# Sparse attention and two feed-forward layers on one core: tying every instruction to its place in the recorded plan

## Chip, cores and metric

The kernel runs on one core of a Trainium2 chip. The metric is the device time of one execution in microseconds (us). The engines are called as the profile calls them: PE (TensorE), ACT (ScalarE), DVE (VectorE), POOL (GpSimd) and SP (SyncE, which here only issues DMA).

## What is computed

The reference takes q, k, v of shape 4 x 8 x 576 x 64 (batches, heads, positions, width) and four weight matrices. Cut to what matters:

```python
scores = np.matmul(q, k.transpose(0, 1, 3, 2)) / np.sqrt(D)
kth = np.partition(scores, -32, axis=-1)[..., -32:-31]       # 32nd largest of each row
scores = np.where(scores >= kth, scores, -1e9)
attn = softmax(scores)
x = (attn @ v), heads side by side                           # 2304 x 512
h = x @ moe_w_in;   x = np.maximum(0.01 * h, h) @ moe_w_out  # 512 -> 2048 -> 512
h = x @ moe2_w_in;  out = (h * sigmoid(h)) @ moe2_w_out
```

## The kernel before

The 2304 tokens are cut into 18 blocks of 128 rows (two of them join the 64 last rows of two batches). In each block the eight heads are done as four pairs, so there are 72 pairs.

One pair goes through all engines in turn. PE multiplies q and k (`S`, line 727); ACT copies the scores out of PSUM (`s_copy`, tile `sb`, line 739); DVE finds the 32nd largest value of each row by seven steps for each of two heads (`chain`, lines 753 to 757: maximum of eight, replace them, and again); ACT masks (`cut`, 779), takes the exponential (`exp`, 788) and writes an fp16 copy (`p_hi`, tile `ph`, 803); POOL writes the rest that fp16 lost (`p_lo`, 811); SP issues a transposing DMA (`ptr`, tile `pT`, 820); PE multiplies with v (`pv`, 841). There are two `sb` buffers, one `ph`, one `pT` and one PSUM tile `S`, so a step waits for a step of an earlier pair that still holds its buffer.

After two pairs ACT and DVE combine the halves of `pv` (`comb_a`, 875, and `comb_b`, 880), and POOL scales them (`comb_c`, 887). After four pairs the block is a row of x, is split into fp16 high and low parts and transposed (`xhi`, `xlo`, `xtr`). Each of the two layers then makes four quanta `h` for a block, of 12 matmuls each (963). A quantum of layer 0 is read by ACT (`g0`, 974); one of layer 1 by ACT (`g1`, a tanh, 976) and then by DVE (`g2`, 981). There are two PSUM tiles `h`, so PE's next quantum waits until one was read. `ghi` (ACT, 990), `glo` (POOL, 997) and `gtr` (SP, 1002) make the transposed input of four quanta `o` (1016), which add up in PSUM tile `acc` (two of them). Layer 0's `acc` becomes y (`ysq`, `yhi`, `ylo`, `ytr`); layer 1's is scaled by ACT (`of`, 1029) and stored. The q and k, v tiles of later pairs are loaded and split on the way (`qsq`, `qsc`, `qhi`, `qtr` and others). In the first 250 us the four weight matrices are also turned from fp64 into two fp16 parts, on DVE, ACT and POOL (`wz`, `wsign`, `wmid`, `wjoin`, `whi`, `wlo`).

What sets the order: each step is an `Op` with its engine and an estimated duration, recorded by `Plan.add`. `Plan.run` (below) schedules all of them by a list scheduler with its own clocks and yields `order`. Its last two lines call every step's function in that order, which traces the instructions:

```python
        for o in order:
            o.fn()
```

That is not yet the order on the engines. When the `TileContext` is closed, the framework's own scheduler goes over the traced instructions. [...]

Of the kernel before, what the change touches and what calls it, by code (L numbers as in the profile page):

```python
# [64 lines left out]
STATS = {}  # L65


class Op:
    __slots__ = ("n", "eng", "dur", "lat", "dma", "fn", "new", "use", "pred", "succ", "bl", "left", "ready", "t0", "t1", "name", "soft", "stage", "slot")


class Plan:
# [5 lines left out]

    def __init__(self):
        self.ops = []
        self.writer = {}
        self.readers = defaultdict(list)
        self.tag = {}
        self.users = defaultdict(list)
        self.last = {}
        self.named = {}

    def add(self, eng, dur, fn, r=(), w=(), new=(), lat=0.0, dma=0.0, seq=None, name="", after=(), mark=None, soft=None, stage=None):  # L90
        o = Op()
        o.n, o.eng, o.dur, o.lat, o.dma, o.fn, o.name = len(self.ops), eng, dur, lat, dma, fn, name
        o.pred, o.succ, o.new, o.use = {}, [], list(new), set()
        for tag, key in new:
            self.tag[key] = tag
        for x in r:
            if x in self.writer:
                o.pred[self.writer[x]] = True
            self.readers[x].append(o)
        for x in w:  # L100
            if x in self.writer:
                o.pred[self.writer[x]] = True
            for y in self.readers[x]:
                if y is not o:
                    o.pred[y] = True
            self.readers[x] = []
            self.writer[x] = o
        for x in list(r) + list(w):
            key = x[0] if isinstance(x[0], tuple) else x
            if key in self.tag and o not in self.users[key]:  # L110
                self.users[key].append(o)
                o.use.add(key)
        for p in after:
            if p in self.named:
                o.pred.setdefault(self.named[p], False)
        if mark is not None:
            self.named[mark] = o
        if seq is not None:
            if seq in self.last:
                o.pred.setdefault(self.last[seq], False)  # L120
            self.last[seq] = o
        o.soft, o.stage, o.slot = None, stage, ()
        if soft is not None:
            if soft in self.last:
                self.last[soft].soft = o
            self.last[soft] = o
        self.ops.append(o)
        return o

    def run(self):  # L130
# [20 lines left out]
        order = []  # L151
# [5 lines left out]
        while len(order) < total:  # L157
            best = None
            for e in engines:
# [25 lines left out]
                x = min((x for x in lst if x[0] <= t0 + SLACK[e]), key=lambda x: (-x[1].bl - BOOST.get(x[1].name, 0), x[1].n))  # L185
# [4 lines left out]
            _, o, t = best  # L190
# [43 lines left out]
                    cand[s.eng].append(s)  # L234
            order.append(o)
        STATS.update(order=order, busy=busy, span=max(o.t1 for o in order))
        for o in order:
            o.fn()


def stages(nb):

    out = []
    for b in range(nb + LEAD):
        if b < nb:
            out.append((0, b))
        if b >= LEAD:
            out.append((1, b - LEAD))
    return out
# [3 lines left out]
def topk_attention_moe_moe2_kernel(  # L253
# [52 lines left out]
    for s in range(NS):  # L306
        blk, p = divmod(s, NP)
        for _, _, b, _ in blocks[blk]:
            first_use.setdefault((b, p), s)

    plan = Plan()
    add = plan.add
    T = {}

# [58 lines left out]
    def w_ops(i):  # L373
# [3 lines left out]
        for c in range(NWP):  # L377
# [3 lines left out]
            for o, n in units:  # L381
# [12 lines left out]
                def load(o=o, n=n, c=c, small=small, rk=rk, raw=raw):  # L394
# [4 lines left out]
                    nc.sync.dma_start(out=dst, in_=w_rows(i, c, o, n))  # L399

                add("SP", 0.55, load, w=rnames, new=rnew, lat=1.8, dma=3.0 * n / WP, name=f"wload{i}", seq="wload",
                    after=W_AFTER if i == 0 and c == 0 else ())

# [3 lines left out]

                zn = [yslot, (yslot, o)] if small else [yslot]
                add("ACT", act_t(n, 1), z, r=rnames, w=zn, name=f"wz{i}")
                m = n if i < 3 else min(n, 512)  # L410
                for o2 in range(0, n, m):
# [12 lines left out]
                    def sign(o2=o2, m=m, tk=tk, t_of=t_of, raw=raw):  # L424
# [8 lines left out]
                        else:  # L433
                            nc.vector.tensor_scalar(u[:, :, 1], s16[:, o2:o2 + m], 32768, None, op0=ALU.bitwise_and)

                    add(W_SIGN[i], {"DVE": 0.08 + 0.65 * m / WP, "POOL": POOL_TS * m / WP}[W_SIGN[i]], sign, r=rnames, w=tn, new=tnew, name=f"wsign{i}")

                    def mid(o2=o2, m=m, t_of=t_of, raw=raw):
# [604 lines left out]
    order = stages(NB)  # L1043
# [62 lines left out]
```

## Time and profile before

| | |
|---|---|
| median of three runs | 1258.48 us (1257.63 to 1261.75) |
| the profiled execution, its own time | 1260.39 us |
| its span, first to last instruction | 1258.6 us |
| busy, share of the span: PE, DVE, ACT, POOL | 81%, 74%, 66%, 49% |
| mean granted TensorE clock | 0.906 |

The span is 1.8 us under the execution's own time. A busy share is an average over stages: the last 150 us are PE alone, the first 250 us are mostly DVE and ACT. An engine runs its instructions in the order in which they stand, so a wait of one instruction is a wait of all behind it; what matters is what stands there.

### The profile page before, as it was taken

How to read it: one execution, taken by the hardware profiler on the slowest of the kernel's cores; microseconds unless marked ns; L12 is line 12 of the kernel's file. 1: busy time of each engine (PE TensorE's matmuls, PEld its weight loads, DVE VectorE, ACT ScalarE, POOL GpSimd, SP SyncE). 2: the span in 40 equal slices, each digit the busy share in tenths (PEclk: the TensorE clock that was granted, in tenths of full speed). 3: DMA queues.
4: the chain of work that ended last, by engine and by line, in shares of the span. 5: the costliest groups of instructions: out<-in, count | busy, mean ns of one | idle time of the engine just before them, and what ended most of it. 6: DMA issues, size and time to landing. Idle time of an engine off the chain costs nothing.

```text
span 1258.6 us, 18096 instructions
## 1 busy us (share of the span) xinstructions
PE 1020.8 (81%) x6024; PEld 503.6 (40%) x6024; DVE 935.6 (74%) x1906; ACT 836.5 (66%) x1408; POOL 616.3 (49%) x864
## 2 busy tenths in 40 slices
PE   3324275798898998897988988989997998999988
PEld 1223133343444443343444433445443443444433
DVE  6989999998749899788788877873988787920000
ACT  6898998887658775676777666665767655642222
POOL 2333455775636554555554645555555544542221
PEclk9555578798999999899989988999999999999989
DMA  8988855456756656467665637565566555553232
GB/s 226 280 247 279 242 135 110 92 97 134 123 117 124 121 117 99 87 123 141 132 111 109 123 73 131 106 132 120 91 118 115 86 100 100 108 114 67 51 74 52
DMA packets 458110, 157.44 MB, mean 125 GB/s; under 512 B 440864, under 2 KB 449056, under 8 KB 455968
## 3 DMA queue, kind: packets, MB, share of 16 engines
q1 hardware_dynamic: 458016, 156.29, 59.7%
q8 instruction: 47, 0.77, 0.3%
q14 instruction: 47, 0.39, 0.1%
HBM read 47.71 MB, written 4.72 MB: 42 GB/s over the span
## 4 chain that ended last, share of the span: by engine, by line
PE 30%; DVE 12%; POOL 10%; DMA 10%; ACT 9%; issue 8%; SPq 1%; POOLq 0%; ACTq 0%; DVEq 0%
PE acc L1016 13%; PE h L963 13%; DMA pT<-ph 5%; DVE w L755 5%; POOL ph L811 5%; DVE m L757 3%; DMA gT<-hl 3%; PE pv L841 2%; ACT sb L739 2%; POOL hl L997 2%; PE S L727 2%; DVE m L753 2%; ACT sb L788 2%; ACT sb L779 1%; ACT ph L803 1%
## 5 line engine op out<-in xcount | busy, mean ns | idle before, releaser
L1016 PE MATMUL acc<-w_all,gT 128*128 128x512 f16 x1728 | 410.7, 390 | 34.0 <-ACT of L1029 19.7
L757 DVE MAX8 m<-w 128x8 f32<-128x576 f32 x432 | 309.6, 749 | 0.1
L997 POOL TENSOR_TENSOR hl<-g,hl 128x512 f16<-128x512 f32 x144 | 168.8, 1173 | 230.5 <-ACT hl L990 208.6
L1016 PEld LDWEIGHTS <-gT 128*128 128x128 f16 x1728 | 168.9, 100 | 239.1 <-issue 52.9
L811 POOL TENSOR_TENSOR ph<-sb,ph 128x1152 f16<-128x1152 f32 x72 | 171.5, 2382 | 129.2 <-ACT ph L803 115.9
L963 PE MATMUL h<-w_all,xT 128*128 128x512 f16 x864 | 207.9, 394 | 21.2 <-ACT g L974 16.7
L963 PE MATMUL h<-w_all,yT 128*128 128x512 f16 x864 | 203.6, 388 | 17.3 <-DVE g L981 15.9
L755 DVE MATCH_REPLACE8 w<-m,w 128x576 f32<-128x576 f32 x288 | 212.4, 743 | 0.0
L753 DVE MAX8 m<-sb 128x8 f32<-128x576 f32 x144 | 103.3, 750 | 76.1 <-ACT sb L739 76.0
L981 DVE SCALAR_TENSOR_TENSOR g<-g,h 128x512 f32<-128x512 f32 x72 | 49.1, 682 | 139.8 <-ACT g L976 139.8
L990 ACT ACTIVATE hl<-g 128x512 f16<-128x512 f32 x144 | 89.7, 624 | 75.4 <-DMA gT<-hl 65.2
L963 PEld LDWEIGHTS <-xT 128*128 128x128 f16 x864 | 86.5, 101 | 128.3 <-issue 34.3
L963 PEld LDWEIGHTS <-yT 128*128 128x128 f16 x864 | 85.7, 100 | 121.3 <-issue 26.7
L739 ACT ACTIVATE sb<-S 128x1152 f32<-128x1152 f32 x72 | 81.2, 1127 | 78.8 <-POOL ph L811 75.8
L727 PE MATMUL S<-k,qT 128*128 128x64 f16 (+3 forms) x640 | 95.8, 309 | 44.2 <-ACT sb L739 37.1
L779 ACT ACTIVATE sb<-sb,m 128x576 f32<-128x576 f32 x144 | 106.1, 766 | 33.2 <-DVE m L757 33.1
L788 ACT ACTIVATE sb<-sb,nb,u 128x576 f32<-128x576 f32 x144 | 123.3, 858 | 5.0 <-POOL nb L767 4.6
L841 PE MATMUL pv<-v,pT 128*128 128x128 f16 (+3 forms) x1600 | 111.7, 213 | 13.8 <-DMA pT<-ph 13.8
L803 ACT ACTIVATE ph<-sb 128x1152 f16<-128x1152 f32 x72 | 83.2, 1156 | 50.5 <-DMA pT<-ph 50.5
L841 PEld LDWEIGHTS <-pT 128*128 128x128 f16 (+3 forms) x1600 | 86.1, 102 | 52.9 <-DMA pT<-ph 18.9
L755 DVE MATCH_REPLACE8 w<-m,sb 128x576 f32<-128x576 f32 x144 | 106.0, 743 | 0.0
L472 PE MATMUL acc<-w_all 128*128 128x128 bf16 x256 | 31.7, 295 | 73.8 <-DVE w_all L455 69.5
(94 smaller groups left out, 1088.4 us busy)
## 6 DMA issues: line engine op xcount, KB each, us to landing
w_all<-in_moe_w_in_dram SPq DMA_DIRECT2D x16, 1024.0 KB, 6.5
w_all<-in_moe_w_out_dram SPq DMA_DIRECT2D x14, 1024.0 KB, 5.1
raw<-in_k_dram SPq DMA_DIRECT2D x16, 256.0 KB, 3.1
rawq<-in_q_dram SPq DMA_DIRECT2D x32, 128.0 KB, 2.8
raw<-in_v_dram SPq DMA_DIRECT2D x16, 256.0 KB, 3.0
out_dram<-of SPq DMA_DIRECT2D x16, 256.0 KB, 2.3
gT<-hl SPq DMA_TRANSPOSE x144, 3.2
of<-in_moe_w_out_dram SPq DMA_DIRECT2D x8, 256.0 KB, 2.8
```

The source lines that it names most:

```text
L727: nc.tensor.matmul(out=t[p0:p1, o:o + k1 - k0], lhsT=lhs, rhs=kt[:, k0:k1], start=(x == 0), stop=(x == 1),)
L739: nc.scalar.activation(out=T[sbk], in_=src, func=AF.Copy)
L753: nc.vector.max(m[:, 0], T[sbk][:, h])
L755: nc.vector.match_replace(w, m[:, step // 2], T[sbk][:, h] if step == 1 else w, NEG)
L757: nc.vector.max(m[:, step // 2], w)
L779: nc.scalar.activation(out=x, in_=x, func=AF.Prelu, scale=-1.0, bias=T["m", s][:, h, 3, 7:8], alpha=2.0**-CUT)
L788: nc.scalar.activation(out=x, in_=x, func=AF.Exp, scale=T["u", blk, hf][:, 1, p % 2:p % 2 + 1], bias=T["nb", s][:, h:h + 1], accum_out=T[" ...
L811: nc.gpsimd.tensor_tensor(out=T[phk][:, 1, x0 * S:x1 * S], in0=T[sbk][:, x0:x1].rearrange("p h k -> p (h k)"), in1=T[phk][:, 0, x0 * S:x1 ...
L841: nc.tensor.matmul(out=o[p0:p1, h, p % 2, 0:n], lhsT=l, rhs=r, start=(i == 0), stop=(i == len(mm) - 1))
L963: nc.tensor.matmul(out=t, lhsT=a[:, ai], rhs=w_rhs(layer, wi, kk, i), start=(n == 0), stop=(n == 3 * KDM - 1))
L997: nc.gpsimd.tensor_tensor(out=n[:, 1], in0=T[gk], in1=n[:, 0], op=ALU.subtract)
L1016: nc.tensor.matmul(out=t, lhsT=g[:, ai], rhs=w_rhs2(layer, wi, 4 * i + j), start=(i == 0 and j == 0 and n == 0), stop=(i == NCH - 1 and j ...
```

## The change

Each traced instruction gets a manual dependency on the instruction that was traced before it on the same engine (`add_manual_dep`, class `NoSync`). Both are on one engine, which keeps their order anyway, so the dependency needs no semaphore: it only binds the framework's scheduler. `use` of an `Op` becomes a list in place of a set. The whole diff:

```diff
--- before.py
+++ after.py
@@ -65,6 +65,9 @@
 STATS = {}
 
 
+ORDER = mybir.DependencyInfo(mybir.DependencyClass.NoSync, mybir.DependencyReason.DATA)
+
+
 class Op:
     __slots__ = ("n", "eng", "dur", "lat", "dma", "fn", "new", "use", "pred", "succ", "bl", "left", "ready", "t0", "t1", "name", "soft", "stage", "slot")
 
@@ -78,7 +81,8 @@
 
 
 
-    def __init__(self):
+    def __init__(self, tc):
+        self.tc = tc
         self.ops = []
         self.writer = {}
         self.readers = defaultdict(list)
@@ -90,7 +94,7 @@
     def add(self, eng, dur, fn, r=(), w=(), new=(), lat=0.0, dma=0.0, seq=None, name="", after=(), mark=None, soft=None, stage=None):
         o = Op()
         o.n, o.eng, o.dur, o.lat, o.dma, o.fn, o.name = len(self.ops), eng, dur, lat, dma, fn, name
-        o.pred, o.succ, o.new, o.use = {}, [], list(new), set()
+        o.pred, o.succ, o.new, o.use = {}, [], list(new), []
         for tag, key in new:
             self.tag[key] = tag
         for x in r:
@@ -109,7 +113,7 @@
             key = x[0] if isinstance(x[0], tuple) else x
             if key in self.tag and o not in self.users[key]:
                 self.users[key].append(o)
-                o.use.add(key)
+                o.use.append(key)
         for p in after:
             if p in self.named:
                 o.pred.setdefault(self.named[p], False)
@@ -234,8 +238,16 @@
                     cand[s.eng].append(s)
             order.append(o)
         STATS.update(order=order, busy=busy, span=max(o.t1 for o in order))
+        behind = {}
         for o in order:
+            traced = self.tc.nc.cur_bb.bb.instructions
+            n = len(traced)
             o.fn()
+            for x in self.tc.nc.cur_bb.bb.instructions[n:]:
+                p = behind.get(x.engine)
+                if p is not None:
+                    self.tc.add_manual_dep(x, p, ORDER, reason="order of issue")
+                behind[x.engine] = x.name
 
 
 def stages(nb):
@@ -308,7 +320,7 @@
         for _, _, b, _ in blocks[blk]:
             first_use.setdefault((b, p), s)
 
-    plan = Plan()
+    plan = Plan(tc)
     add = plan.add
     T = {}
```

No instruction is added or taken away. Names of buffers carry the numbers that tracing gave them; they are the same in both programs, so the plan is the same. In the program of before the engines' order differs from the plan; in the changed one it is the plan. PE's order is nearly the same in both from the end of the weight work on: of its 11942 rows 11003 stand at the same place. On ACT, DVE, POOL and SP most places differ. Lines of the changed kernel are 12 higher in this part (739 becomes 751).

**First place, ACT and DVE in block 13 of layer 1.** ACT before; `g_10495` is `g1` of the layer's first quantum of that block, read from PSUM tile `h_10427`, and `xf_10509` is `comb_a`:

```order
L739 ACTIVATE sb_10471<-S_10385 128x1152
L779 ACTIVATE sb_10362<-sb_10362,m8_10402 128x576 x2
L788 ACTIVATE sb_10362,rs_10002<-sb_10362,nb_10512,u_9631 128x576 x2
L990 ACTIVATE hl_10556<-g_10383 128x512
L990 ACTIVATE hl_10614<-g_10424 128x512
L976 ACTIVATE g_10495<-h_10427,u2_10274 128x512
L976 ACTIVATE g_10568<-h_10451,u2_10274 128x512
L875 ACTIVATE xf_10509<-pv_10310 128x256
```

And now:

```order
L751 ACTIVATE sb_10471<-S_10385 128x1152
L988 ACTIVATE g_10495<-h_10427,u2_10274 128x512
L887 ACTIVATE xf_10509<-pv_10310 128x256
L791 ACTIVATE sb_10362<-sb_10362,m8_10402 128x576 x2
L800 ACTIVATE sb_10362,rs_10002<-sb_10362,nb_10512,u_9631 128x576 x2
L1002 ACTIVATE hl_10556<-g_10383 128x512
L1041 ACTIVATE of_10560<-acc_10341,u2_9597 128x512
```

`g1` and `comb_a` stood behind two `cut`, two `exp` and two `ghi`, and now stand right behind `s_copy` (`sb_10471`). DVE there, before (`g_10495` is `g2`, `xf_10509` is `comb_b`, the rows on `m8_10534` are the chain of the next pair):

```order
L753 MAX m8_10534<-sb_10471 128x8 x2
L755 MATCH_REPLACE w_10535<-m8_10534,sb_10471 128x576 x2
L757 MAX m8_10534<-w_10535 128x8
L856 SCALAR_TENSOR_TENSOR den_10563<-rs_10002,sv3_78 128x4
L757 MAX m8_10534<-w_10535 128x8
L862 RECIPROCAL rec_10565<-den_10563 128x4
L755 MATCH_REPLACE w_10535<-m8_10534,w_10535 128x576 x2
L981 SCALAR_TENSOR_TENSOR g_10495<-g_10495,h_10427 128x512
L757 MAX m8_10534<-w_10535 128x8 x2
L755 MATCH_REPLACE w_10535<-m8_10534,w_10535 128x576
L981 SCALAR_TENSOR_TENSOR g_10568<-g_10568,h_10451 128x512
L880 TENSOR_TENSOR xf_10509<-pv_10310,xf_10509 128x256
```

And now:

```order
L993 SCALAR_TENSOR_TENSOR g_10495<-g_10495,h_10427 128x512
L892 TENSOR_TENSOR xf_10509<-pv_10310,xf_10509 128x256
L765 MAX m8_10534<-sb_10471 128x8 x2
L767 MATCH_REPLACE w_10535<-m8_10534,sb_10471 128x576 x2
L868 SCALAR_TENSOR_TENSOR den_10563<-rs_10002,sv3_78 128x4
L874 RECIPROCAL rec_10565<-den_10563 128x4
L769 MAX m8_10534<-w_10535 128x8 x2
L767 MATCH_REPLACE w_10535<-m8_10534,w_10535 128x576
L993 SCALAR_TENSOR_TENSOR g_10568<-g_10568,h_10451 128x512
L767 MATCH_REPLACE w_10535<-m8_10534,w_10535 128x576
L769 MAX m8_10534<-w_10535 128x8 x2
```

Both `g2` and `comb_b` stood inside the chain, and now stand ahead of its first row.

**Second place, ACT in block 9 of layer 0.** `g_7092` is the `g0` for which a quantum of `h` waits. Before (`xss_7035`, `hlx_7102` are `ysq`, `yhi`; `qss_7147` is `qsq`):

```order
L990 ACTIVATE hl_7196<-g_6909 128x512
L974 ACTIVATE g_6993<-h_6941 128x512
L901 ACTIVATE junk_69,xss_7035<-acc_6775 128x512
L650 ACTIVATE junk_69,qss_7147<-rawq_7067 128x256
L922 ACTIVATE hlx_7102<-acc_6775,ys_7054 128x512
L803 ACTIVATE ph_7128<-sb_6870 128x1152
L779 ACTIVATE sb_7014<-sb_7014,m8_7063 128x576 x2
L974 ACTIVATE g_7092<-h_7041 128x512
L739 ACTIVATE sb_7168<-S_7026 128x1152
```

And now:

```order
L751 ACTIVATE sb_7014<-S_6900 128x1152
L913 ACTIVATE junk_69,xss_7035<-acc_6775 128x512
L1002 ACTIVATE hl_7038<-g_6845 128x512
L791 ACTIVATE sb_6870<-sb_6870,m8_6931 128x576
L677 ACTIVATE rawq_6935<-rawq_6935,qs_7020 128x256
L791 ACTIVATE sb_6870<-sb_6870,m8_6931 128x576
L986 ACTIVATE g_7092<-h_7041 128x512
L800 ACTIVATE sb_6870,rs_6933<-sb_6870,nb_7090,u_6067 128x576
L934 ACTIVATE hlx_7102<-acc_6775,ys_7054 128x512
L800 ACTIVATE sb_6870,rs_6933<-sb_6870,nb_7090,u_6067 128x576
L815 ACTIVATE ph_7128<-sb_6870 128x1152
```

`g0` stood behind `ysq`, `qsq`, `yhi`, `p_hi` and the two `cut` of `sb_7014`. Of these only `ysq` is still ahead of it. It now stands right behind the `cut` of the pair before (`sb_6870`), and that pair's two `exp`, which ran long before it, stand behind it.

**Third place, SP in block 5.** `pT_4669` is the transpose `ptr` for which a `pv` waits. Before:

```order
L939 DMA_TRANSPOSE yT_4589<-hlx_4588 128x8x128
L1002 DMA_TRANSPOSE gT_4616<-hl_4615 128x8x128
L692 DMA_TRANSPOSE qT_4679<-hlx_4678 128x8x128
L820 DMA_TRANSPOSE pT_4669<-ph_4592 128x18x128
L1002 DMA_TRANSPOSE gT_4649<-hl_4648 128x8x128
L641 DMA rawq_4746<-in_q_dram 128x4x64
```

And now:

```order
L951 DMA_TRANSPOSE yT_4589<-hlx_4588 128x8x128
L832 DMA_TRANSPOSE pT_4669<-ph_4592 128x18x128
L1014 DMA_TRANSPOSE gT_4616<-hl_4615 128x8x128
L1014 DMA_TRANSPOSE gT_4649<-hl_4648 128x8x128
L704 DMA_TRANSPOSE qT_4679<-hlx_4678 128x8x128
L653 DMA rawq_4746<-in_q_dram 128x4x64
```

`ptr` stood behind a `gtr` (`gT_4616`) and a `qtr`; now it is ahead of both.

## Rows read from the trace of the kernel before

**Rows 1.** Busy time on the page: us (share of the span) xinstructions.

```profile
PE 1020.8 (81%) x6024; PEld 503.6 (40%) x6024; DVE 935.6 (74%) x1906; ACT 836.5 (66%) x1408; POOL 616.3 (49%) x864
```

**Rows 2.** Three stretches: length, busy us (instructions) by engine, granted clock, DMA share, GB/s.

```profile
0.00:250.00 250.00, 116.19 (x751) 69.29 (x752) 227.62 (x425) 214.88 (x311) 114.66 (x144) 0.69 0.73 202
250.00:1105.00 855.00, 760.84 (x4580) 368.87 (x4579) 692.03 (x1458) 576.82 (x1021) 462.83 (x671) 0.96 0.61 113
1105.00:1259.00 154.00, 143.81 (x697) 65.40 (x695) 15.92 (x26) 44.82 (x77) 38.77 (x49) 0.98 0.36 70
```

**Rows 3.** Waits of PE, 250 to 1105 us: us in total, times, longest us.

```profile
PE acc L1016 <- ACT of L1029: 19.7, 9, 5.7
PE h L963 <- ACT g L974: 16.7, 6, 5.8
PE h L963 <- DVE g L981: 15.9, 6, 5.8
PE S L727 <- ACT sb L739: 11.4, 11, 2.6
PE pv L841 <- DMA pT<-ph: 11.2, 7, 3.5
PE h L530 <- DVE g L981: 5.0, 1, 5.0
```

**Rows 4.** Timeline of ACT near 1053 us: start, us, instruction, [idle before <-releaser].

```profile
1052.41 1.13 ACT L739 ACTIVATE sb<-S 128x1152 f32<-128x1152 f32 x1 [1.66 <-POOL ph L811]
1053.44 1.43 ACT L779 ACTIVATE sb<-sb,m 128x576 f32<-128x576 f32 x2
1054.77 0.86 ACT L788 ACTIVATE sb<-sb,nb,u 128x576 f32<-128x576 f32 x1
...
1055.62 0.86 ACT L788 ACTIVATE sb<-sb,nb,u 128x576 f32<-128x576 f32 x1
...
1056.47 1.14 ACT L990 ACTIVATE hl<-g 128x512 f16<-128x512 f32 x2
1057.52 0.67 ACT L976 ACTIVATE g<-h,u 128x512 f32<-128x512 f32 x1
```

**Rows 5.** Timeline of PE in the same stretch.

```profile
1045.74 5.34 PE L963 MATMUL h<-w_all,yT 128*128 128x512 f16 x24
...
1060.00 1.33 PE L963 MATMUL h<-w_all,yT 128*128 128x512 f16 x4 [2.67 <-DVE g L981]
```

**Rows 6.** Timeline of ACT and PE near 730 us.

```profile
724.04 0.86 ACT L788 ACTIVATE sb<-sb,nb,u 128x576 f32<-128x576 f32 x1
...
724.50 5.34 PE L963 MATMUL h<-w_all,xT 128*128 128x512 f16 x24
...
733.26 0.69 ACT L922 ACTIVATE hlx<-acc,ys 128x512 f16<-128x512 f32 x1 [5.30 <-POOL ys L330]
...
734.90 1.43 ACT L779 ACTIVATE sb<-sb,m 128x576 f32<-128x576 f32 x2
...
736.23 0.58 ACT L974 ACTIVATE g<-h 128x512 f32<-128x512 f32 x1
...
736.86 4.15 PE L963 MATMUL h<-w_all,xT 128*128 128x512 f16 x12 [5.85 <-ACT g L974]
```

**Rows 7.** Timeline of the SP queue near 495 us.

```profile
494.58 1.23 SPq L1002 DMA_TRANSPOSE gT<-hl  x1
495.92 2.01 SPq L692 DMA_TRANSPOSE qT<-hlx  x1
498.03 3.19 SPq L820 DMA_TRANSPOSE pT<-ph  x1
```

**Rows 8.** Timeline of PE near 500 us.

```profile
502.72 1.33 PE L841 MATMUL pv<-v,pT 128*128 128x128 f16 x20 [3.55 <-DMA pT<-ph]
```

**Rows 9.** Waits of DVE, 250 to 1105 us.

```profile
DVE g L981 <- ACT g L976: 42.8, 18, 13.8
```

**Rows 10.** Waits of ACT, 250 to 1105 us.

```profile
ACT g L974 <- PE h L963: 10.0, 6, 4.2
```

## The prediction

> **What bounds the kernel now.** I read first the page's busy time, then the same by stage, then what PE waits for, then the order at the worst waits. On the page [rows 1] PE is busy for 1020.8 us of 1258.6, DVE for 935.6: no engine is full, so the shares alone do not tell the bound. The three stretches do [rows 2]. In the first 250 us DVE is busy for 227.6 and ACT for 214.9: the weights are made, and PE has little to do at a granted clock of 0.69. In the last 154 us PE is busy for 143.8 and DVE for 15.9: the attention is done, and PE works off what is left. Between them, 855 us, PE is busy for 760.8 and DVE for 692.0. What PE does not do in the middle it must do in the end, so PE's idle time of the middle, 855 - 760.8 = 94.2 us, is what a better order can win, as long as the chain on DVE keeps up; DVE has 855 - 692.0 = 163 us of slack there.
>
> The list of PE's waits in the middle [rows 3] says what the 94 us are. Most are not for data but for a place to write: PE waits for ACT to empty `acc` (`of`, 19.7 us in 9 waits), for ACT or DVE to empty an `h` tile (16.7 in 6, 15.9 in 6, and 5.0 once in front of a small matmul that takes an `h` tile too). That is 57.3 us in 22 waits. 11.2 us are waits for the transposed probabilities, 11.4 for `s_copy`.
>
> **What the order does there.** First place: PE ends two quanta of `h` at 1045.74 + 5.34 = 1051.1, so the first at about 1048.4, and stands still for 2.67 us until 1060.00, when `g2` has freed that tile [rows 5]. ACT could have run `g1` from 1048.4 on, but `s_copy`, two `cut`, two `exp` and two `ghi` stood ahead, and it ran at 1057.52 [rows 4]. Now it stands right behind `s_copy`, which ends at 1052.41 + 1.13 = 1053.5: four us earlier, more than the 2.67 that PE lost. On DVE `g2` now comes ahead of the next pair's chain, which starts later by about the two steps that moved.
>
> Second place: `g0` ran at 736.23 and PE waited 5.85 us for it [rows 6]. Its `h` was ready by 724.50 + 5.34 / 2 = 727.2; ACT then stood 5.30 us in front of `yhi`. Now `g0` is ahead of `yhi`, and the wait is gone. But its new place is ahead of an `exp` that ran at 724.04. At the times of this trace ACT would stand there for 727.2 - 724.04 = 3.2 us, with the pair's exponentials behind it. This is the price of the change, and it shows the risk.
>
> Third place: `ptr` was issued at 498.03, behind a `gtr` and a `qtr` of 1.23 and 2.01 us [rows 7], and PE waited 3.55 us for its landing [rows 8]. Now it goes ahead of both: 3.2 us earlier.
>
> **The change part by part.**
> - *Waits for a free PSUM tile*, 57.3 us [rows 3]. At two of two places read, the awaited step passes more work than PE lost. Yet these are the worst places of the old order, and a new one has worst places of its own. Bounds: 0 and -57.3. I take half: -28.7.
> - *Waits for `pT`*, 11.2 us [rows 3], by the third place: bounds 0 and -11.2, I take half: -5.6.
> - *The clock after a wait.* [...] Bounds: 0, and -34 us, the 0.04 that the middle's granted clock of 0.96 lacks [rows 2], times 855.
> - *New waits at the head of ACT and DVE.* They show already: DVE stood 42.8 us for `g1` [rows 9], ACT 10.0 us for `h` [rows 10], 52.8 together. PE-fed steps now stand earlier, so I let these waits double. What stands behind is the chain and its `cut` and `exp`; these reach PE as waits for `pT` and `s_copy`, 11.2 + 11.4 = 22.6 of PE's 94 us, a quarter. 52.8 / 4 = +13.2. Bounds: 0 and +52.8, all of it passed on.
> - *The first 250 us.* Weight steps on DVE move ahead of steps of the first chains. The same work runs on an engine busy for 227.6 of 250 us, so one gains what the other loses: 0, with DVE's idle 22 us [rows 2] as bound on either side.
> - *The last 154 us.* PE's order is unchanged and PE is busy for 143.8 [rows 2]: 0, at best -10.
> [...]
>
> Sum: -28.7 - 5.6 - 7.5 + 13.2 = -28.6 us. Against the profiled execution's own 1260.4 us this is 1231.8; that execution lies 1.9 us above the median of the runs, 1258.5, so I forecast **1230 us**.
>
> [...]
>
> **The rivals.**
> - *Slower: the heads block.* ACT and DVE start nothing ahead of the instruction at their head. In the middle some 15 blocks pass with eight `g`, two `comb_a` and one `of` each, 165 PE-fed steps on ACT, all with the pair's `cut` and `exp` behind them. If PE comes no earlier than in this trace, they wait as in the second place, there for 3.2 us. With 0.8 us on average ACT stands 132 us longer, of its idle 855 - 576.8 = 278 [rows 2]; half of it reaching the pair's loop is +66, less the 41.8 us won above: +24, **1283 us**. It decides from 0.5 us on average (165 x 0.5 / 2 = 41). For it: the 3.2 us, and 42.8 us that DVE stood in the same way [rows 9]. Against it: 10.0 us in 6 waits is all that ACT stood for layer 0's `h` [rows 10], and PE itself comes earlier when its tiles come free. [...]
> - *No change.* PE's order is nearly the same, and PE soon comes to the next `S` or `pv`, which hang on the chain. Then a wait for a free tile becomes a wait for `s_copy` or `pT`, and the time stays: **1258 us**. To the same comes the case that the change does not act: the framework's order might differ only where nobody waits. The three places speak against that.
> [...]
>
> **How the numbers follow.** Forecast (1205 to 1254): 0.53. Much faster: 0.11. No change: 0.11. Slower: 0.25. A measurement of this kernel tells about 0.3%, 3.8 us, from no change; the chances are faster 0.64, same 0.11, slower 0.25. The range leaves out half of the much faster case and about a half of the slower one, whose price grows with each tenth of a us of mean wait: 1193 to 1284 us.
>
> **What would show it.** Right: in the middle stretch PE's waits for `of`, `g0` and `g2` fall from 57 to about 30 us, its granted clock rises above 0.96, and the last chain ends before 1105 us. The new price: ACT's waits for `h` and DVE's for `g1` grow from 52.8 towards 100. Wrong: PE's idle time in the middle stays at 94 us and only changes its name to `s_copy` and `pT`, or ACT stands for `h` for well over 100 us and the chain ends after 1105.

## The result and the profile after

The changed kernel takes **1146.95 us** (median of four runs, 1143.96 to 1147.79) against 1258.18 us before (1257.63 to 1261.75): the ratio is 0.911, 95% interval 0.908 to 0.913. That is 111 us less, where the prediction had 28.6, and 46 us below its range. The sign was right, the size was not. The profiled execution took 1143.96 us with a span of 1142.2, 116.4 us under the span of before.

One thing stated ahead has to be put right: there is one PSUM tile `acc`, not two. So a wait for `of` is a wait for the only tile there is. Lines of the changed kernel are 12 higher: 963 is 975, 974 is 986, 976 is 988, 739 is 751.

The page's busy line after, to hold against [rows 1]:

```profile
PE 986.2 (86%) x6024; PEld 497.1 (44%) x6024; DVE 931.5 (82%) x1906; ACT 839.9 (74%) x1408; POOL 622.6 (55%) x864
```

The instructions are the same in number, and in both traces they run in the order of the built programs: all 1159 ACTIVATE rows of ACT and all 498 DMA issues of SP stand at their place. DVE, ACT and POOL need the same time for them within about 1%, PE 34.6 us less (1020.8 - 986.2). Now the three stretches after, cut where the last chain ends on DVE (before: 1105 us; now 997):

```profile
0.00:250.00 250.00, 112.24 (x735) 68.03 (x736) 225.72 (x421) 214.16 (x305) 119.53 (x142) 0.83 0.71 201
250.00:997.00 747.00, 736.87 (x4630) 366.54 (x4629) 691.02 (x1463) 583.74 (x1032) 465.80 (x677) 1.00 0.71 129
997.00:1143.00 146.00, 137.13 (x663) 62.49 (x660) 14.77 (x23) 42.01 (x73) 37.30 (x47) 1.00 0.37 72
```

Against [rows 2]: the first 250 us are as they were but for PE's granted clock there (0.69 before, 0.83 now), the last stretch is 8 us shorter, and the middle is 108 us shorter with the same work on DVE (692.0 and 691.0 us). In it PE is busy for 736.87 of 747 us, 98.6%, at a granted clock of 1.00, where it was 0.96 before. The 116.4 us of span can be written as PE's busy time plus its idle time by stretch (the end up to the last instruction):

| PE | before | after | difference |
|---|---|---|---|
| busy, all | 1020.8 | 986.2 | -34.6 |
| idle, first 250 us | 133.8 | 137.8 | +4.0 |
| idle, middle | 94.2 | 10.1 | -84.1 |
| idle, end | 9.8 | 8.1 | -1.7 |

What PE waits for in the middle, 250 to 997 us, to hold against [rows 3] (us in total, times, longest):

```profile
PE h L542 <- ACT junk L598: 3.2, 2, 2.8
PE acc L1028 <- ACT of L1041: 3.1, 2, 2.4
PE pv L853 <- DMA pT<-ph: 1.5, 2, 0.9
PE S L739 <- ACT sb L751: 1.3, 2, 1.1
```

The waits for `g0` and `g2` are gone from the list; 3.1 us for `of`, 1.5 for `pT` and 1.3 for `s_copy` are left. The price that the prediction looked for stands in the lists of DVE and ACT of the same stretch. DVE and ACT after:

```profile
DVE g L993 <- ACT g L988: 8.9, 13, 3.8
...
DVE m L765 <- ACT sb L751: 3.6, 5, 2.1
...
ACT sb L751 <- POOL ph L823: 38.8, 42, 2.0
ACT g L986 <- PE h L975: 25.0, 22, 3.9
ACT g L988 <- PE h L975: 22.0, 24, 3.5
...
ACT xf L887 <- PE pv L853: 11.3, 9, 2.2
```

ACT now stands for `h` 47.0 us (25.0 for `g0`, 22.0 for `g1`). Before it was 11.5: the 10.0 of [rows 10] are `g0` alone, and `g1` adds 1.5 (last line below). DVE stands for `g1` 8.9 us, not 42.8 [rows 9]. Some rows of before that the prediction did not read belong beside them (DVE and ACT, 250 to 1105 us):

```profile
DVE m L753 <- ACT sb L739: 73.9, 38, 5.8
...
ACT sb L739 <- POOL ph L811: 67.2, 45, 3.3
ACT ph L803 <- DMA pT<-ph: 50.0, 26, 4.8
...
ACT g L976 <- PE h L963: 1.5, 4, 0.7
```

DVE's wait for the scores at the head of the chain was the largest wait of DVE before, and fell from 73.9 to 3.6 us. The whole loop of a pair (`s_copy`, chain, `p_hi`, `p_lo`, `ptr`) became quicker, with every step as long as it was. That this one wait falls is no gain in itself, as the kernel with only DVE tied shows below.

The second place of the prediction shows how a new wait costs nothing. ACT and PE after, with the same `g0` (start, us, instruction, idle before it):

```profile
662.50 5.34 PE L975 MATMUL h<-w_all,xT 128*128 128x512 f16 x24
...
663.95 0.76 ACT L791 ACTIVATE sb<-sb,m 128x576 f32<-128x576 f32 x1
665.35 0.60 ACT L986 ACTIVATE g<-h 128x512 f32<-128x512 f32 x1 [0.64 <-PE h L975]
...
667.68 1.32 PE L853 MATMUL pv<-v,pT 128*128 128x128 f16 x20
```

The quantum of `h` is ready at about 662.50 + 5.34 / 2 = 665.2, and `g0` follows at once. ACT stood for 0.64 us, not for the 3.2 that the times of the old trace gave, because PE came earlier too. PE's next rows follow without a gap.

### The profile page after: what moved, and what is told of

It is laid out like the page before. It is cut to its first block, busy times and chain, and to the rows that moved or that the text cites. A ratio compares the mean times of both kernels' runs of the same rounds, so it can differ in the third digit from the quotient of the medians.

```text
span 1142.2 us, 18088 instructions
## 1 busy us (share of the span) xinstructions
PE 986.2 (86%) x6024; PEld 497.1 (44%) x6024; DVE 931.5 (82%) x1906; ACT 839.9 (74%) x1408; POOL 622.6 (55%) x864
## 4 chain that ended last, share of the span: by engine, by line
PE 68%; ACT 8%; DVE 7%; DMA 6%; issue 5%; POOL 3%; SPq 1%; POOLq 0%; ACTq 0%; DVEq 0%
PE h L975 28%; PE acc L1028 28%; PE pv L853 7%; PE S L739 5%; DVE w L767 2%; DVE m L769 1%; DVE w_all L467 1%; DMA w_all<-in_moe_w_in_dram 1%; ACT w_all L418 1%; ACT sb L800 1%; ACT w_all L458 1%; DMA raw<-in_k_dram 1%; DMA w_all<-in_moe_w_out_dram 1%; POOL ph L823 1%; DMA gT<-hl 1%
## 5 line engine op out<-in xcount | busy, mean ns | idle before, releaser
L1028 PE MATMUL acc<-w_all,gT 128*128 128x512 f16 x1728 | 398.4, 381 | 7.6 <-ACT of L1041 3.1
L1028 PEld LDWEIGHTS <-gT 128*128 128x128 f16 x1728 | 166.0, 99 | 203.3 <-issue 11.8
L975 PE MATMUL h<-w_all,xT 128*128 128x512 f16 x864 | 200.6, 385 | 2.1 <-DMA xT<-hlx 1.8
L975 PE MATMUL h<-w_all,yT 128*128 128x512 f16 x864 | 196.8, 379 | 0.1
L853 PEld LDWEIGHTS <-pT 128*128 128x128 f16 (+3 forms) x1600 | 85.9, 101 | 46.3 <-DMA pT<-ph 11.5
L988 ACT ACTIVATE g<-h,u 128x512 f32<-128x512 f32 x72 | 49.3, 684 | 73.4 <-PE h L975 63.7
L779 POOL TENSOR_SCALAR nb<-m,u 128x1 f32<-128x1 f32 x144 | 67.7, 473 | 62.2 <-DVE m L769 50.1
```

What stands on the lines that cost most here:

```text
L853: nc.tensor.matmul(out=o[p0:p1, h, p % 2, 0:n], lhsT=l, rhs=r, start=(i == 0), stop=(i == len(mm) - 1))
L975: nc.tensor.matmul(out=t, lhsT=a[:, ai], rhs=w_rhs(layer, wi, kk, i), start=(n == 0), stop=(n == 3 * KDM - 1))
L1028: nc.tensor.matmul(out=t, lhsT=g[:, ai], rhs=w_rhs2(layer, wi, 4 * i + j), start=(i == 0 and j == 0 and n == 0), stop=(i == NCH - 1 and j ...
```

## Experiments

How far a step stands off its place in the plan is counted in instructions of its engine, from the built programs, as a mean over the whole kernel. In the kernel before, `g0`, `g1`, `of` stand 3.5 to 4.2 places late, `comb_a` 5.4, `g2` 4.8, `comb_b` 6.6, `s_copy` 0.9, `p_hi` 1.6, `p_lo` 2.2 and `ptr` 2.0; `qsq` 3.7, `qhi` 6.3 and `qsc` 7.1 places early.

The theories:
- **A**: the steps that empty PE's tiles (`g0`, `g1`, `of`, `comb_a`; `g2`, `comb_b` on DVE) came late. This is the prediction's mechanism.
- **B**: steps of q, k and v were drawn forward on ACT and stood at its head for data that was not there.
- **C**: DVE's order decides, since DVE carries the chain.
- **D**: the pair's own path (`p_hi`, `p_lo`, `ptr`, `s_copy`) came late.

Each run has its own runs of the kernel before on the same chip; their medians lie between 1258.2 and 1260.6 us. Differences below are against the change's 1146.95 us; one of 2 or 3 us says nothing.

### Whose order is it?

Eight kernels tie only some engines. The edit is one condition:

```diff
             for x in self.tc.nc.cur_bb.bb.instructions[n:]:
+                if not (o.eng in ("ACT",)):
+                    continue
                 p = behind.get(x.engine)
```

**Only ACT tied** (the edit above).

> Only ACT's instructions are tied to the plan; the framework places the rest (on DVE g2 and comb_b still 3 places late). Theory A (steps that empty PE's tiles came late on ACT): most of the 111 us is won, 1150 to 1175 us, and PE's waits for of, g0 and g2 in the middle are under 20 us. Theory B (steps of q, k and v drawn forward on ACT held up the pair's path): the same time, but PE's waits for s_copy and pT are what is gone. Theory C (DVE's order decides): 1220 to 1260 us.

Measured: 1189.8 us (ratio 0.945, 0.940 to 0.949). ACT's order alone gives 69 of the 111 us, 15 us short of the range that I gave to A and B. PE's waits in its middle (250 to 1000 us) answer as A has it: those for `of` (1.7 us) and `g0` are nearly gone and none for `g2` is left, while those for `s_copy` and `pT` stay. DVE still waits for the scores too (28.5 us where the change has 3.6).

```profile
PE S L741 <- ACT sb L753: 10.2, 12, 2.0
PE pv L855 <- DMA pT<-ph: 9.6, 9, 2.1
PE h L977 <- ACT g L988: 2.7, 2, 1.6
```

**Only DVE tied**: `o.eng in ("DVE",)`.

> Only DVE's instructions are tied; on ACT the steps that empty PE's tiles stand 2 to 3 places late and the steps of q 6 to 9 places early, much as before. Theory A: 1210 to 1250 us, with most of the 57 us of PE's waits for free tiles back. Theory B: 1210 to 1250 us too, with DVE waiting some 50 us for s_copy. Theory C: 1150 to 1175 us.

Measured: 1257.6 us (0.998, 0.996 to 1.000). Theory C falls: DVE's order by itself gives nothing. DVE's wait for the scores did shrink (73.9 us before; 8.8 here, 250 to 1000 us), but DVE stands for `g1` in its place:

```profile
DVE g L995 <- ACT g L990: 60.1, 24, 13.5
...
DVE m L767 <- ACT sb L753: 8.8, 5, 2.5
```

**All but DVE**: `o.eng != "DVE"`. `g2` stands 2.7 and `comb_b` 3.4 places late, the chain 1.7 to 2.1 early.

> All tied but DVE, where g2 and comb_b stand 3 places late and the chain 1.5 places early. Theory A: 10 to 30 us slower, 1155 to 1175 us, with PE's waits for g2 at 5 us or more. Theory B: within 10 us, 1140 to 1157 us. With ACT alone tied it was 1189.8 us: if DVE's order is what was missing there, this comes near it.

Measured: 1154.2 us (0.917, 0.915 to 0.920), 7 us more than the change, less than A had it.

**All but ACT**: `o.eng != "ACT"`.

> Every engine but ScalarE tied; ScalarE's instructions stand where the framework puts them: g0, g1, of and comb_a 2 to 3 places late, p_hi 1.7, cut and exp 1.2, the steps of q 4 to 5 places early. ScalarE's order tied by itself gave 68 of the 111 us, so theories A and B (steps that empty TensorE's tiles late on ScalarE; steps of q early on it) give 1200 to 1250. If the other engines carry as much of the gain when they are all tied: 1165 to 1195.

Measured: 1259.8 us (1.001, 0.999 to 1.002). Without ACT's order nothing at all is left of the gain, though four engines run the plan; A and B had let me expect 1200 to 1250. It also shows that `use` as a list, which this kernel has too, is not the cause. PE's waits in its middle (250 to 1000 us) are for ACT again, but not in the old shares: `s_copy` leads with twice its 11.4 us, `of` follows, and `g0` and `g2` are small (3.8 and 3.1 us):

```profile
PE S L741 <- ACT sb L753: 24.2, 16, 6.3
PE acc L1030 <- ACT of L1043: 15.3, 6, 4.9
```

So ACT's order alone is worth 69 us, that of all the others without it nothing, all together 111. I asked next which engine adds the 43 that ACT alone lacks.

**ACT and DVE**: `o.eng in ("ACT", "DVE")`.

> ScalarE and VectorE tied, GpSimd, SyncE and TensorE left to the framework. ScalarE alone took 1189.8, all but VectorE 1154.2, all 1147. If GpSimd's or SyncE's own order carries the 36 us between the first two: 1180 to 1195. If those engines only follow the other two (so that any engine beside ScalarE brings them into line): 1145 to 1160.

Measured: 1175.7 us (0.934, 0.925 to 0.943; two runs, 1172.9 and 1178.4): 14 less than ACT alone, 29 more than all, and between my two cases. DVE's order is not all that ACT's lacked.

**All but POOL**: `o.eng != "POOL"`.

> All tied but GpSimd, whose instructions then stand 0.7 places off the plan on average. If they follow the other engines: 1145 to 1155. If GpSimd's places are as dear as they seemed in late_prob: 1165 to 1200.

Measured: 1152.9 us (0.916, 0.909 to 0.923), 6 more. POOL mostly follows the others.

**All but SP**: `o.eng != "SP"`.

> All tied but SyncE, whose transposes then stand 0.4 places off the plan on average, the probabilities' 0.3 late. late_ptr, with these up to 2 places late, cost 180 us, so 0.3 places are some 27 by proportion. If SyncE's own order carries the 29 us that ScalarE and VectorE tied alone leave: 1165 to 1180. If another engine holds it in line: 1145 to 1156.

Measured: 1159.8 us (0.921, 0.916 to 0.926), 13 more, half of what I expected and between the two theories.

**ACT and SP**: `o.eng in ("ACT", "SP")`.

> ScalarE and SyncE tied, the rest left to the framework. ScalarE alone took 1189.8, ScalarE and VectorE 1175.7, all but VectorE 1154.2. If SyncE's order is the second term: 1152 to 1168. If GpSimd or any two together are needed: 1175 to 1190.

Measured: 1178.4 us (0.936, 0.927 to 0.944; 1174.7 and 1182.0). SP's order adds 11 us to ACT's, as DVE's adds 14. Neither of the two carries the 43 us; ACT with POOL was not tried. Beside all the rest each costs little when it is loose (7 us for DVE, 6 for POOL, 13 for SP), so most of the 43 us comes when any two of the three hold beside ACT. One thing is mixed in: PE is loose where ACT is tied with one engine, and tied where all but one are. From the first `h` of layer 1 on, PE's order differs from the plan there in some 350 of about 10,500 instructions. PE's order was not tried by itself, so its share is not known.

### Which stretch is it?

**Tied only up to the first `h` of layer 1**, about the first 250 us:

```diff
+        start = next(i for i, o in enumerate(order) if o.name == "h1")
-        for o in order:
+        for at, o in enumerate(order):
...
+                if not at < start:
+                    continue
```

> Tied only as far as the first tiles of h of the second layer (about the first 250 us); after that the framework's order on every engine. If the gain lies in the middle, made by the order there: 1248 to 1268. If a better start makes the middle fast: 1150 to 1200.

Measured: 1260.7 us (1.001, 1.000 to 1.002). The order of the first 250 us gives nothing; the gain is made in the middle by the order there.

### Which steps are it?

These kernels tie all engines and move named steps out of the plan's order by up to so many places of their engine, as far as data and buffers allow:

```diff
+        order = shifted(order, {"g0": 8, "g1": 8, "of": 8, "comb_a": 8, "g2": 10, "comb_b": 10})
         behind = {}
```

**Steps that empty PE's tiles, late** (the edit above). They come out 3.0 to 3.5 places late (`comb_a` 2.1, `of` 1.3, `comb_b` 1.4).

> All tied, but g0 and g1 are put 3 places later on ACT than in the plan, comb_a 2, of 1, and g2 3 places later on DVE; all else keeps its order. Theory A: 25 to 60 us slower than the changed kernel, with PE's waits for of, g0 and g2 at 20 us or more. Theory B: under 10 us slower, 1145 to 1157 us. Theory C: some 20 us slower, with the chain earlier and g2 later.

Measured: 1204.7 us in one execution; a second took 2604 us and is left out, so there is no interval. That is 58 us more. PE's waits in its middle name them:

```profile
PE acc L1047 <- ACT of L1060: 14.4, 6, 3.7
PE h L994 <- ACT g L1005: 11.5, 11, 2.8
...
PE h L994 <- DVE g L1012: 6.0, 9, 1.4
```

**The same, one place late**: every number in the table is 1; 0.7 to 0.9 places come out.

> All tied, but g0, g1, of, comb_a, g2 and comb_b one place (0.7 to 0.9 on the mean) later. With 3 places it was 58 us. Theory A with a price in proportion: 10 to 20 us slower, 1155 to 1168 us. If PE runs far enough ahead to hide one place: within 4 us of the changed kernel.

Measured: 1158.1 us (0.920, 0.918 to 0.923), 11 more. One place costs 11 us, three cost 58 (one execution): late readers do cost time, as A has it, the price grows with lateness, and the plan has no room of a whole place.

**Steps of q early on ACT**: `{"qsq": -7, "qsc": -7, "qhi": -7}`; they come out 4.7 to 5.4 places early, their loads and transposes stay. The pair's steps on ACT thereby stand 0.3 (`s_copy`) to 0.9 places (`p_hi`) later.

> All tied, but the q steps qsq, qsc and qhi are put 5 to 6 places earlier on ACT; all else keeps its order. Theory A: under 10 us slower, 1145 to 1157 us. Theory B: 25 to 60 us slower, with ACT standing for POOL's qscale or for the transposes of q, and DVE waiting 30 us or more for s_copy.

Measured: 1266.8 us (1.006, 1.004 to 1.008), 120 more, twice what B had let me expect; the whole gain is lost. ACT stood for loads that had not landed, and PE for the `s_copy` behind them (both 250 to 1000 us):

```profile
ACT junk L681 <- DMA rawq<-in_q_dram: 49.2, 20, 4.1
...
PE S L758 <- ACT sb L770: 41.8, 22, 5.6
```

This shows that such a head can cost that much. It overstates B, since in the kernel before the loads had moved forward as well: there ACT stood only 5.2 us for them.

**Steps of q, k, v left to the framework**, with their loads and transposes; all else tied: `not (o.name[0] == "q" or o.name[:2] == "kv" or o.name in ("ktr", "factor"))`. The framework puts the steps of q 6.5 to 12 places early on ACT. What they pass comes later by that: `g0` and `g1` 1.5 places, `s_copy` 1.6, `p_hi` 2.1, `ptr` 2.4.

> All tied but the steps of q, k and v with their loads and transposes, which the framework now puts 8 to 12 places earlier on ACT and earlier on SP, as in the kernel before; all else keeps its order and stands 1.5 to 2 places later by that. Theory A (late emptying of PE's tiles): 15 to 45 us slower than the changed kernel, 1160 to 1190 us. Theory B (ACT stands at the head of q's steps): 80 to 120 us slower, 1225 to 1265 us, with ACT's waits for q's loads, for POOL's qscale and for transposes at 40 us or more in the middle.

Measured: 1210.4 us (0.962, 0.959 to 0.965), 63 more, between my two ranges. PE waits 20.8 us for `s_copy` there, where [rows 3] has 11.4. So B, with all that it pushes back, costs about as much as A. The two prices, 58 and 63, add to more than the 111 us, and neither kernel has its steps just where the kernel before had them, so they are not shares of the gain.

That B was at work in the kernel before, its trace shows: ACT stood 36.6 us at the head for steps of q (`qsc` 665, `qhi` 673, `qsq` 650; 250 to 1105 us). After the change 0.2 us of this are left.

```profile
ACT rawq L665 <- POOL qs L330: 15.3, 12, 3.3
...
ACT hlx L673 <- DMA xT<-hlx: 9.7, 5, 4.0
...
ACT hlx L673 <- DMA qT<-hlx: 6.4, 7, 2.6
ACT junk L650 <- DMA rawq<-in_q_dram: 5.2, 5, 2.3
```

### The pair's own path

**`p_hi`, `p_lo`, `ptr` and `s_copy` late**: `{"s_copy": 1, "p_hi": 2, "p_lo": 2, "ptr": 2}`; 0.8 places and three times 2.0 come out.

> All tied, but p_hi stands 2 places later on ACT, p_lo 1.5 on POOL, ptr 2 on SP and s_copy 0.8, as far as they stood in the kernel before; all else keeps its order. Theory A: under 15 us slower, up to 1162 us. Theory D (the pair's own way from exp to the next s_copy decides): 30 us or more slower, with DVE's waits for s_copy back at 40 us or more.

Measured: 1393.7 us (1.108, 1.102 to 1.114), 247 more, the largest price of all: 3.4 us for each of the 72 pairs.

**ACT's part of it alone**: `{"s_copy": 1, "p_hi": 2}`; 0.8 and only 0.9 places come out, since `p_lo` and `ptr`, which need `p_hi`, stay.

> All tied, but on ScalarE p_hi 2 places and s_copy 1 place later in every pair; p_lo on GpSimd and ptr on SyncE stay. late_prob, with all four later, took 1393.7. If ScalarE's part makes that loss: 1245 or more. If GpSimd's and SyncE's part does: 1165 to 1210.

Measured: 1175.1 us (0.932, 0.929 to 0.936), 28 more.

**SP's part of it alone**: `{"ptr": 2}`; 1.9 places come out.

> All tied, but the transpose of the probabilities up to 2 places later on SyncE in every pair; ScalarE and GpSimd as in the change. late_prob took 1393.7 and late_phi 1175.1: the 219 us between them are p_lo's 1.5 places on GpSimd and this transpose's on SyncE. If SyncE's part makes them: 1250 or more. If GpSimd's does: 1147 to 1180.

Measured: 1327.6 us (1.055, 1.046 to 1.063), 181 more. Of the engines' waits in its middle (250 to 1000 us) one row each shows the way, the SP queue, ACT, POOL and PE in turn:

```profile
SPq L1033 <- POOL hl L1028: 75.7, 26, 7.6
...
ACT ph L834 <- DMA pT<-ph: 101.0, 43, 5.1
...
POOL ph L842 <- ACT ph L834: 183.2, 47, 8.2
...
PE pv L872 <- DMA pT<-ph: 72.3, 36, 8.6
```

A `gtr` (line 1033) stands at the head of SP and waits for `glo` on POOL; the `ptr` behind it waits too. There is one buffer `ph`, so the next pair's `p_hi` waits on ACT until `ptr` has read it: 101 us, where the change has 2.3 us in 3 waits. Behind `p_hi` stands all of ACT, and POOL waits for `p_hi`. The same loop ran in the kernel before, with `ptr` 2.0 places late: the 50.0 us of `ACT ph L803` above. A second `ph` buffer was not tried, nor `p_lo` by itself; the 38 us between 28 + 181 and 247 can come from `p_lo`, from the second place of `p_hi`, or from both together.

So A, B and D each cost time by themselves, and all three were there in the kernel before. What each had of the 111 us is not shown: their prices add to far more.

### A better order?

**Two other sets of the plan's tables** (due times, boosts, slacks, and the weights' sign and low parts on other engines), all tied. The first, cut to its core:

```diff
-W_SIGN = ("DVE", "DVE", "DVE", "DVE")
-W_LO = (("DVE", "ACT"),) * 4
+W_SIGN = ("POOL", "DVE", "DVE", "POOL")
+W_LO = (("ACT", "POOL"), ("DVE", "ACT"), ("DVE", "ACT"), ("DVE", "ACT"))
...
```

> All tied as in the change, with other due times, boosts and slacks in the plan's tables (and the weights' sign and low parts given to other engines), so that the written order itself differs. If TensorE is the bound and full from 256 us on, only the first 250 us and the end can give: 1120 to 1145. If the order of the change is already as good as the chip lets it be, or the tables fit the plan's costs and not the chip's: 1147 to 1180.

Measured: 1143.5 us (0.907, 0.904 to 0.911). The interval overlaps that of the change (0.908 to 0.913), so the two are not told apart. PE's busy time in the first 250 us is 109.3 us, no more than the change's 112.2, though POOL took over work of DVE.

The second, with `W_SIGN = ("POOL", "POOL", "DVE", "DVE")` and `AHEAD = 3`:

> All tied, with a third set of due times, boosts and slacks in the plan's tables. plan_s5 took 1143.5, the change 1147. If the first 250 us and the end still have something to give: 1125 to 1143. If any sound order gives the same within 1%: 1140 to 1155.

Measured: 1154.0 us (0.917, 0.910 to 0.924), 7 more. Neither beats the change clearly. Of PE's 156 idle us after the change 138 lie in the first 250 us; what would bring PE to work earlier there stays open.

## Why the prediction was wrong

The mechanism was right as far as it went: the steps that PE waits for stand earlier on ACT, DVE and SP, the middle shrinks, and PE's waits and its clock are what shrinks. The sizes were wrong where I chose a value between two bounds, and a part of the mechanism had no term.

| step of the prediction | taken | its bound | measured |
|---|---|---|---|
| waits for a free PSUM tile | -28.7 | -57.3 | -54.2 (57.3 to 3.1) |
| waits for `pT` | -5.6 | -11.2 | -9.7 (11.2 to 1.5) |
| clock after a wait | -7.5 | -34 | -34.6 (PE's busy time, whole kernel) |
| new waits at the heads of ACT and DVE | +13.2 | +52.8 | no wait of PE found for them |
| first 250 us | 0 | 22 either way | +4 idle on PE |
| last 154 us | 0 | -10 | -8 (154 to 146) |

The rows overlap: 6.7 of the last 8 us are busy time of PE, which the clock's row counts too.

- **"I take half" is the step that failed**, twice: for the tiles and for `pT`. Its reason was that the places read were the worst of the old order and that a new order has worst places of its own. After the change 3.1 us are left for `of` and none for `g`. The plan was made so that each reader stands where PE's product falls due, and the one-place experiment (11 us, `of` 6.9 us in 4 waits) shows how close. Three worst places could not tell it; the mean displacement over all steps could: 3.5 to 6.6 places late for every reader. By the later run (one execution) about three places are worth 58 us.
- **The clock** was mis-sized: the -7.5 of the sum is a term that no run shows. In the kernel before, the quantum behind the 5.85 us wait [rows 6] ran at a granted clock of 0.65 on the mean (736.86 to 741.01 us), the two ahead of the wait at 1.00 (724.50 to 729.84 us). With the waits nearly all gone, the middle's granted clock rose from 0.96 to 1.00, and PE's busy time fell by 34.6 us: the bound, all of it. Here it was no small second term: it went whole with the waits.
- **The new waits** came, in part: ACT's for `h` grew from 11.5 to 47.0 us, DVE's for `g1` fell from 42.8 to 8.9; together 54.3 before and 55.9 after, where the prediction had 52.8 and looked for 100. Passing a quarter of them on, +13.2, was wrong. ACT waited for PE, and PE was the bound and full; ACT had 747 - 583.7 = 163 us of idle time for it. I take it that a wait at a head costs where what stands behind it is late for the bound engine, as in the run with early steps of q (49.2 us of waits for loads, 120 us lost). There ACT waited for something that was not the bound.
- **Missing from the sum** was a part of the change. The prediction spoke of readers that stood late; steps of q, k and v that stood early were in its second place (`qsq` ahead of `g0`) but had no term. Left to the framework, with all that they push back, they cost 63 us, and in the kernel before ACT stood 36.6 us for them. PE's waits for `s_copy` were only used to find a share to pass on, as if they would stay; they fell from 11.4 to 1.3 us. The chain kept up: DVE is busy for 93% of the middle, 81% before. The 163 us of slack that I read were enough for it; 56 are left.
- **The rivals.** *The heads block*: fell; ACT's waits for `h`, for `pv` (`comb_a`) and for `acc` (`of`, 3.8 us) are 62.1 us, over 165 steps 0.38 us, under the point of 0.5 from which it decides, and even these did not reach PE, which stands idle for 10.1 us in all. *No change*: fell; the waits did not change their name. *Much faster* (0.11) was nearest: the range's lower end of 1193 us leaves out half of it, and the change lies 46 us below that end. The bounds themselves (-57.3 - 11.2 - 34 - 10, and 11.4 for `s_copy`) add to -124, near the 116.4 us that the span lost.
- **PE as the bound** was read rightly from the stretches. After the change its matmuls fill 98.6% of the middle, while its weight loads are 366.5 of 747 us, 49%; by the weight loads alone PE would not have looked full. With PE full, the middle is as long as PE's work. That DVE at 93% is not the engine to relieve is argued from this; no run gave DVE less to do there.

## What to carry to other kernels

When a plan and the order that runs differ, count over the whole program how many places each kind of step is off, on every engine, and price the kinds that the bound engine waits for; three bad places show the sign but not the size. Test an engine's order both alone and as the only one missing: here ACT alone gave 69 of 111 us, and all engines but ACT gave none. When every wait in a list has one cause, take the list's whole sum and the slow clock that goes with it (here 34.6 us of PE's busy time), and halve it only for a reason that a row shows.

## What was not expected of the hardware

Two places of one transposing DMA of each pair on SP's queue cost 181 us, more than the whole change gained, while three places of all readers of PE's tiles cost 58. The queue holds the transpose behind one that is not ready, and through the only `ph` buffer the delay comes back to ACT's head: 101 us in 43 waits between 250 and 1000 us.

The clock added to each large loss. In the middle of the run with the late transposes it was granted at 0.93, and PE was busy for 1038.1 us with the same matmuls that took 986.2 in the change: 52 of the 181 us are slower matmuls and not waits. Against the change, PE's idle time and its busy time over the whole span grew together: by 82 and 35 us in the kernel before, by 131 and 52 with the late transposes, by 180 and 67 with the whole path late, so by 0.37 to 0.42 us of busy time for each us of idle time. Where less idle time came back, the ratio was not steady (0.1 to 0.8). These are windows of the run with the late transposes:

```profile
250.00:1000.00 750.00, 656.39 (x3936) 319.92 (x3935) 583.11 (x1238) 499.60 (x881) 399.79 (x584) 0.93 0.59 110
...
sum 1390.00, PE 1038.10 PEld 508.08 DVE 937.75 ACT 840.23 POOL 622.93; mean PE 346.03 PEld 169.36 DVE 312.58 ACT 280.08 POOL 207.64
```
